# A gated sum of two attentions on one core: two turned operands, the weight loads, two scratch layouts and filling matmuls changed together

## The chip, the cores and the metric

The kernel runs on one core of a Trainium2 chip. The metric is the device time of one execution in microseconds (us). Three runs of the kernel before gave 1566.88, 1573.17 and 1576.6 us, so the median is 1573.17 us. The profiled execution took 1573.35 us; its span, from its first to its last instruction, is 1571.6 us.

## The reference, cut to what matters

Both attentions read the same x (2048 tokens of 576 values, bfloat16) and their results are mixed token by token by a gate g.

```python
# A: 32 heads of 128, 64 segments of 32 tokens, one after the other
for s in range(64):
    h = concat([mem, x[:, 32*s:32*s+32]])          # 8 + 32 = 40 rows
    q, k, v = h @ Wq, h @ Wk, h @ Wv                # 576 -> 32 x 128 each
    p = softmax(where(mask, q @ k.T * scale, -1e9))  # 40 x 40 per head
    o = (p @ v) @ Wo                                # 40 x 576
    mem = o[:, :8]                                  # the next segment needs this
    outs.append(o[:, 8:])
# B: full attention, 32 heads of 18, 2048 x 2048 scores per head
b = softmax(q_b @ k_b.T * scale_b) @ v_b @ wo
return g * a + (1 - g) * b                          # g = sigmoid((x * gate_w).sum(-1))
```

## The kernel before, in words

**The order of work.** Nothing is scheduled by the framework. Every piece of work is an `Op` with an engine (or a choice of two), an estimated duration, the pieces it depends on, a priority, and buffers ("tokens") that it takes and gives back. The class `Plan` (lines 45 to 204) runs a list scheduler over these estimates and emits the instructions of each engine in the order it finds. Its priorities are the numbers in `RANK` (line 17). On the chip each engine then works through its own list in order, and an instruction that waits holds up all behind it, on the queue of SP, which issues most DMAs, as well. The plan lets at most 8 DMAs of SP be under way at once.

**Start (before the segments).** x is loaded and turned on TensorE (`x_tile`). `project_qk` (line 532) and `project_v` (line 570) compute B's q, k and v, 36 and 32 products of five matmuls, and store them to DRAM scratch `qtd`, `ktd` and `vgd`; the store of v (line 597) writes pieces of 128 values. Meanwhile POOL issues the loads of A's three weight matrices, twelve groups of one 1024 KB and two 64 KB transfers (`load_w`, lines 477 to 486), each released by the end of the group before the last. `last_unit` (line 792) computes q, k and v of the last 8 tokens of 16 segments at a time, 24 units per 16 segments; the first 24 run before segment 0, the others among the segments. It stores q and k to `qkd` (line 844) in pieces of 32 values and v to `vld`.

**B.** 512 visits: one is 4 row-tiled score matmuls (`visit`, L708) into the only score buffer (4 PSUM banks), one exponential of 128 x 2048 on ScalarE (`expo`, L717), and 4 column-tiled matmuls (`values`, L726) that add to one open bank `ob` over 16 visits. `load_v` (line 671) brings the values back. At the end of the kernel function (lines 1393 to 1399) the visits beyond the first 23 are tied to segments, so that about 7.6 of them go with each.

**A segment.** `project` (line 1016) computes Q, K and V in two halves of 16 heads: six groups (called Q0, K0, Q1, K1, V0, V1 below) of 20 column-tiled matmuls (L1028). Each is copied from PSUM to a tile `tm` (128 x 512) by VectorE or ScalarE; there are four such tiles. For each half, `turn` (line 1082) transposes the Q and the K tile by 8 TensorE matmuls into a PSUM bank `pt`, and `ct` (line 1094) copies that bank to `qk` on VectorE. V is moved from `tm` to `v_sb` by 8 DMAs from SP (`put_v`, L1067). `ld_l` and `put_l` bring the last 8 tokens' q and k from `qkd` into `qk`. Then, per half: scores (`psh`, L1108), exponential on ScalarE, mask, sums, reciprocals, scaling on VectorE with small TensorE products between, values (`pso`, L1172), copies to `ot`, and `out_pieces` (L946), 64 small matmuls per half into `acc`. `ob_cast`, `ob_bd` and `fold` turn the 8 memory rows, and `put_h` (L1227) writes them into `ht` for the next segment: from one `put_h` to the next is the period of the recurrence. `put_o` (L1247, on POOL) collects the last 8 tokens for `last_out`, which multiplies those of four segments at once (again L946).

**End.** A's rows come back from DRAM, POOL multiplies them by g (L1349), TensorE multiplies B's result by its output weights (L1362), and VectorE joins the two.

Of the kernel before, what the change touches and what calls it, by code (L numbers as in the profile page):

```python
# [16 lines left out]
RANK = {  # L17
    "switch": 0.289, "near": 0.006, "early": 0.149, "wait": 0.21, "Q0": 1.449, "K0": 1.44, "Q1": 1.668,
    "K1": 1.703, "V0": 1.816, "V1": 1.981, "t0": 0.855, "t1": 0.104, "ph0": 2.493, "ph1": 1.947, "sm0": 1.698,
    "sm1": 1.765, "bc0": 1.404, "bc1": 1.296, "po0": 0.05, "po1": 0.541, "op0": 1.569, "op1": 0.05,  # L20
    "fo": 1.154, "lo0": 2.104, "lo1": 2.247, "la": 1.796, "ob": 1.008, "eQ": 0.456, "eK": 1.902, "eV": 1.335,
    "co": 3.82, "le": 6.051, "xp": 0.18, "mn": 0.857, "fin": 3.893, "la_gate": 1, "lo_gate": 1, "ahead": 23,
    "behind": 2, "tail": 0.042,
}
# [20 lines left out]
class Plan:  # L45
# [5 lines left out]
    SWITCH = 0.1  # L51

    def __init__(self):
        self.ops = []
        self.tokens = {}
        self.now = None
        self.lanes = [0.0] * self.LANES
        self.moved = 0.0

# [38 lines left out]
    def run(self):  # L98
# [12 lines left out]
        n = len(self.ops)  # L111
        best = {}
        dirty = set(free)
        while len(order) < n:
# [10 lines left out]
            est, op = best[pick]  # L125
            waiting_engs = op.engs
# [6 lines left out]
            if pick == "PE":  # L133
                if op.mode != mode:
                    dur += self.SWITCH
                mode = op.mode
            op.end = est + dur
# [78 lines left out]
def kernel(  # L216
# [68 lines left out]
    nc.vector.memset(cap[:], 3.0e38)  # L285
    nc.vector.memset(bsel[:], 0.0)
# [24 lines left out]
    vgd = dpool.tile([GB, P, NKB * P], BF16, name="vgd")  # L311
    otd = dpool.tile([Dm, S], BF16, name="otd")
    vld = dpool.tile([n_seg * LO, HD], BF16, name="vld")
    qkd = dpool.tile([n_seg // SG, P, SG, 2, H * LO], BF16, name="qkd")
# [22 lines left out]
    wo7 = bint.tile([P, Dm], BF16, name="wo7")  # L337
# [50 lines left out]
    z_w7 = zero("zw7", wo7[:], 0.6, 4.0)  # L388
# [83 lines left out]
    weight_loads = {}  # L472
    chain = [wbl[-1], wbl[-1]]
    for w, src, name in ((wv, A_Wv, "wv"), (wq, A_Wq, "wq"), (wk, A_Wk, "wk")):
        w2 = src.rearrange("d h e -> d (h e)")
        for c in range(NF):
            def load_w(e, w=w, w2=w2, c=c):
                nc.gpsimd.dma_start(out=w[0][:, c, :], in_=rows(w2, c))
                for two in range(2):
                    o = TL * two + TR * c  # L480
                    nc.gpsimd.dma_start(
                        out=w[1][o:o + TR, :],
                        in_=w2[RW * c + P:RW * c + RW, two * (HD // 2):(two + 1) * (HD // 2)],
                    )

            chain.append(add(f"{name}{c}", "POOL", 2.1, load_w, [chain[-2]], prio=0.15, tail=8.5))
        weight_loads[name] = chain[-4:]
# [8 lines left out]
    gwl = add("gw", "POOL", 5.0, load_gw, [chain[5]], prio=0.9, tail=3.0)  # L496
# [35 lines left out]
    def project_qk(which, m, t, prio):  # L532
# [20 lines left out]

        def st(e):
# [15 lines left out]
    def project_v(hf, kb, prio):  # L570
# [24 lines left out]

        def st(e):
            dma(
                out=vgd[:, :, :].rearrange("g p (k f) -> k p g f", f=P)[kb][:, hf * GB // 2:(hf + 1) * GB // 2, :],
                in_=vt[:, :, :].rearrange("p (g j) e -> p g (j e)", j=4),
            )  # L600

        v_stores[k] = add(f"vs{hf}{kb}", "SP", 0.4, st, [b], prio=0.8, dmas=1, kb=260)
# [29 lines left out]
    for m in range(1, 5):  # L632
# [3 lines left out]
        if m == 2:  # L636
            for kb in range(NKB):
                project_v(1, kb, 0.55)
    b_work = [o for o in plan.ops if o.name[:2] in ("pq", "pv", "ga", "xl", "xs")]
# [31 lines left out]
    def load_v(c):  # L671
# [4 lines left out]
        def fn(e):  # L676
            dma(out=vring[c % NVR][:, :], in_=vgd[g, :, kc * QC:(kc + 1) * QC])
# [13 lines left out]
    fin_state = {}  # L691

    for gq in range(GB * NQC):
        g, qc = divmod(gq, NQC)
        load_q(gq)
        for kb in range(NKB):
# [41 lines left out]
            if kb == 0:  # L738
                first_va = va
# [40 lines left out]

# [658 lines left out]
```

## Time and profile before

| | |
|---|---|
| profiled execution, its span | 1573.35 us, 1571.6 us |
| busy in the span: TensorE, ScalarE, VectorE, POOL | 1425.7 us (91%), 1066.2 us (68%), 764.9 us (49%), 194.4 us (12%) |
| mean granted TensorE clock | 0.961 of full speed |
| first and last start of a segment's projection matmul (L1028) | 168.8 us, 1524.8 us |
| median distance of two `put_h` (190.3 to 1514.2 us), smallest, largest | 21.2, 19.2, 24.2 us |
| DMA packets, of them under 512 B | 246877, 186487 |

The rows of groups in the profile give line, engine, operation, output and input tile, shape, number, then busy time and the mean ns of one, and then the idle time of the engine just before them with what ended it. The rows of stretches give, for a window of time, each engine's busy us and number of instructions, then the granted TensorE clock, the share of the DMA engines that were busy, and GB/s. The chain of waits gives start, length, and the engine and line that the end of the program was waiting for at that time; "issue" is time in which the profile shows no wait. Matmuls overlap, so a mean of 391 ns for one of four does not mean that four take 1.6 us.

### The profile page before, as it was taken

The numbers are of one execution on the slowest core, as the hardware profiler recorded it, in microseconds if no ns is written. First come the engines' busy times: TensorE is split into PE (matmuls) and PEld (weight loads), VectorE is DVE, ScalarE is ACT, GpSimd is POOL, SyncE is SP. The second block draws the span as 40 slices with busy tenths as digits, with TensorE's granted clock in tenths as the row PEclk, the third lists the DMA queues.
The fourth block names the chain that finished last, engine by engine and source line by source line (L and its number), as shares of the span: only waits on it lengthen the run. The fifth ranks groups of instructions, "written<-read, shape, count | busy, mean of one in ns | idle before, by whom it ended". The sixth has DMA issues, their size and how long they took to land.

```text
span 1571.6 us, 68445 instructions
## 1 busy us (share of the span) xinstructions
PE 1425.7 (91%) x30582; PEld 813.4 (52%) x30582; DVE 764.9 (49%) x1604; ACT 1066.2 (68%) x809; POOL 194.4 (12%) x523
## 2 busy tenths in 40 slices
PE   5398999999999999999999999999999898988996
PEld 3154545555554545555555555555555454555555
DVE  5154555544545454545554544555444545443454
ACT  2121788877777777777777777777776767766771
POOL 7301000000000000010000000000110100000025
PEclk9599999999999999999999999999999999998998
DMA  9957411212222111222221112212131111111033
GB/s 319 287 152 206 68 44 51 56 33 45 42 49 49 32 44 53 56 43 46 39 50 44 42 43 52 57 39 41 38 76 37 34 34 40 33 32 31 26 106 97
DMA packets 246877, 104.83 MB, mean 67 GB/s; under 512 B 186487, under 2 KB 242039, under 8 KB 245047
## 3 DMA queue, kind: packets, MB, share of 16 engines
q1 hardware_dynamic: 241591, 80.40, 21.2%
q0 software_dynamic: 3840, 18.88, 3.5%
q8 instruction: 239, 3.92, 1.0%
q10 hardware_dynamic: 1152, 1.18, 0.3%
q14 instruction: 55, 0.45, 0.1%
HBM read 52.74 MB, written 30.86 MB: 53 GB/s over the span
## 4 chain that ended last, share of the span: by engine, by line
PE 72%; ACT 10%; DMA 7%; issue 4%; SPq 3%; DVE 3%; POOL 1%; ACTq 0%; DVEq 0%; POOLq 0%
PE pvv L1028 24%; PE acc L946 11%; PE sb L708 10%; ACT etb L717 9%; PE ob L726 8%; PE pt L1087 4%; PE pv L807 4%; DMA v_sb<-tm 3%; SPq L1067 2%; PE pq L539 2%; PE pso L1172 2%; PE pv L803 2%; PE psh L1108 1%; POOL wv_m L1349 1%; PE prb L1151 1%
## 5 line engine op out<-in xcount | busy, mean ns | idle before, releaser
L717 ACT ACTIVATE etb<-sb 128x2048 bf16<-128x2048 f32 x512 | 961.3, 1878 | 386.3 <-PE sb L708 328.2
L363 DVE CAST tm<-pvv 128x512 bf16<-128x512 f32 x352 | 242.6, 690 | 285.2 <-PE pvv L1028 270.9
L1028 PEld LDWEIGHTS <-ht 128*32 128x32 bf16 x7680 | 199.5, 96 | 186.9 <-DVE ht L1227 23.8
L708 PE MATMUL sb<-qch,kch 32*128 32x512 bf16 x2048 | 208.6, 391 | 28.9 <-ACT etb L717 18.0
L726 PE MATMUL ob<-etb,vch 128*32 128x512 bf16 x2048 | 207.4, 396 | 0.8 <-ACT etb L717 0.7
L946 PE MATMUL acc<-wo,ot 128*32 128x144 bf16 x8192 | 167.7, 245 | 10.9 <-issue 10.7
L946 PEld LDWEIGHTS <-ot 128*32 128x32 bf16 x8192 | 157.1, 107 | 22.2 <-issue 17.2
L1028 PE MATMUL pvv<-wk_m,ht 128*32 128x512 bf16 x2048 | 140.8, 380 | 18.3 <-DVE ht L1227 18.2
L1028 PE MATMUL pvv<-wq_m,ht 128*32 128x512 bf16 x2048 | 144.4, 380 | 0.0
L708 PEld LDWEIGHTS <-kch 32*128 32x128 bf16 x2048 | 65.1, 91 | 139.9 <-issue 109.3
L1028 PE MATMUL pvv<-wv_m,ht 128*32 128x512 bf16 x2048 | 133.9, 379 | 0.0
L983 POOL COPY ht<-xg 128x96 bf16<-128x96 bf16 x64 | 17.1, 267 | 859.7 <-PE pvv L1028 843.2
L363 DVE CAST ot<-pso 128x320 bf16<-128x320 f32 x197 | 90.0, 485 | 65.1 <-PE pso L1172 64.8
L1095 DVE COPY qk<-pt 128x1024 bf16<-128x1024 bf16 x128 | 87.8, 686 | 53.8 <-PE pt L1087 53.5
L726 PEld LDWEIGHTS <-vch 128*32 128x32 bf16 x2048 | 54.3, 93 | 112.6 <-issue 105.0
L1203 DVE CAST obf<-acc 128x144 bf16<-128x144 f32 x64 | 19.7, 307 | 169.4 <-PE acc L946 169.2
L1087 PEld LDWEIGHTS <-tm 128*128 128x128 bf16 x1024 | 57.5, 98 | 45.5 <-issue 27.1
L1087 PE MATMUL pt<-ident,tm 128*128 128x128 bf16 x1024 | 79.4, 220 | 0.0
L1172 PE MATMUL pso<-et,v_sb 64*128 64x40 bf16 x2048 | 54.7, 179 | 26.0 <-DVE ot L363 16.8
L1161 DVE TENSOR_TENSOR et<-et,prb 128x320 bf16<-128x320 bf16 x128 | 57.2, 483 | 23.8 <-PE prb L1151 22.1
L1172 PEld LDWEIGHTS <-v_sb 64*128 64x128 bf16 x2048 | 38.8, 94 | 56.3 <-DMA v_sb<-tm 29.0
L1247 POOL COPY otl<-ot 128x256 bf16<-128x256 bf16 x64 | 26.2, 409 | 328.2 <-DVE ot L363 187.8
(128 smaller groups left out, 1523.1 us busy)
## 6 DMA issues: line engine op xcount, KB each, us to landing
v_sb<-tm SPq DMA_DIRECT2D x512, 32.0 KB
qkd<-vl SPq DMA_DIRECT2D x64, 128.0 KB
xl<-qkd SPq DMA_DIRECT2D x64, 128.0 KB
wo<-in_A_Wo_dram POOLq DMA_DIRECT2D x4, 1152.0 KB, 11.3
wv_m<-in_A_Wv_dram POOLq DMA_DIRECT2D x4, 1024.0 KB, 10.6
vgd<-vt SPq DMA_DIRECT2D x32, 128.0 KB
wq_m<-in_A_Wq_dram POOLq DMA_DIRECT2D x4, 1024.0 KB, 10.1
wk_m<-in_A_Wk_dram POOLq DMA_DIRECT2D x4, 1024.0 KB, 12.3
```

The costliest lines, as they stand in the source:

```text
L363: nc.vector.tensor_copy(out=out_of(), in_=in_of())
L539: nc.tensor.matmul(pq[:, :], lhsT=lw(c), rhs=xT[:, c, cs], start=(c == 0), stop=(c == NF))
L708: nc.tensor.matmul(sb[:, j, :], lhsT=kc[r, o:o + P], rhs=qt_[r, :], start=True, stop=True, tile_position=(32 * j, 0),)
L717: nc.scalar.activation(out=etb[:, :, :], in_=box["sb", gq, kb][:, :, :], func=ACT.Exp, scale=scale_b)
L726: nc.tensor.matmul(ob[32 * j:32 * j + 32, :], lhsT=vc[:, o + 32 * j:o + 32 * j + 32], rhs=etb[:, j, :], start=(kb == 0), stop=(kb == NKB - ...
L807: nc.tensor.matmul(pv[:, k * P:(k + 1) * P], lhsT=lw, rhs=xL[:, cc, cols], start=(c == 0), stop=(c == NF))
L946: nc.tensor.matmul(acc[32 * j:32 * j + 32, :], lhsT=o[:, slot, t0:t0 + CT], rhs=wo[:, h, RW * j:RW * j + RW], start=(first and s_ == 0), s ...
L1028: nc.tensor.matmul(pv[32 * j:32 * j + 32, :], lhsT=ht[:, cc, :], rhs=rw, start=(c == 0), stop=(c == NF), tile_position=(0, 32 * j), skip_g ...
L1087: nc.tensor.transpose(out=pt[:, a, :, i, :], in_=tm[:, i * Dh:(i + 1) * Dh], identity=ident[:, :])
L1095: nc.vector.tensor_copy(out=opened["qk"][:, hf, :, 0:16 * L].rearrange("p a (h t) -> p a h t", t=L)[:, :, :, 0:CT], in_=box["pt", s, hf][: ...
L1161: nc.vector.tensor_tensor(out=et[:, :], in0=et[:, :], in1=box["prb", s, hf][:, :], op=ALU.mult)
L1172: nc.tensor.matmul(ps[jj][:, r * L:(r + 1) * L], lhsT=v_sb[rr, hf * 1024 + r * Dh:hf * 1024 + (r + 1) * Dh], rhs=et[rr, r * L:(r + 1) * L] ...
```

## The change

1. **Turning.** The 8 matmuls of `turn` and the copy out of PSUM are replaced, for each of Q and K of each half, by one transposing DMA from SP (`tm` to a new tile `tt`, three of them) and one copy from `tt` to `qk` on VectorE or POOL. There are 4 DMAs and 4 copies in a segment where there were 16 matmuls and 2 copies. A `tm` tile is given back when its DMA is done.
2. **Weights.** The loads of A's weights and of its output weights are released one by one: each waits for a chosen copy of the B projections (or of the first `last_unit`s) through a small VectorE memset into its target.
3. **Scratch.** `vgd` and `qkd` are laid out so that each store writes 1 KB per partition; the load of `vch` then reads pieces of 128 values, and the load of `xl` pieces of 32 values, where they read 1 KB.
4. **Filling.** While `ob` is open, the planner puts a product of a zero tile with a tile of ones, added to `ob`, wherever its own timetable shows TensorE idle for at least 0.216 us (plus 0.1 us if the tiling changes): four column-tiled matmuls of 512 columns, or one full one.
5. **Around it.** All priorities have new numbers. The last block of B's output weights is loaded after the last Q instead of early. One buffer `otl` replaces two, and `last_out` for a group is planned ahead of the next group's `put_o`. `put_h` and `put_x` depend on all six groups of an earlier segment instead of V1 alone. Visits beyond 20 (before: 23) are tied to segments.

```diff
-    "switch": 0.289, "near": 0.006, "early": 0.149, "wait": 0.21, "Q0": 1.449, "K0": 1.44, "Q1": 1.668,
...
+    "switch": 0.401, "near": 0, "early": 0.353, "wait": 0.286, "Q0": 1.145, "K0": 1.449, "Q1": 1.603,
+    "K1": 1.589, "V0": 1.999, "V1": 4.037, "t0": 0.42, "t1": 0.05, "ph0": 6.405, "ph1": 0.336, "sm0": 1.963,
...
+            if pick == "PE" and open_ and self.warm is not None:
+                for m in ("col", "full"):
+                    if m not in (mode, op.mode):
+                        continue
+                    turn = 0.0 if mode == m else self.SWITCH
+                    done = sum(d for t, d in recent if t > free["PE"] - 2.5)
+                    if est - free["PE"] < self.WARM + turn + RANK["gap"] or done > RANK["cool"]:
+                        continue
+                    w = Op("warm", "PE", self.WARM, self.warm[m], [], 9.0, m, (), (), 0.0)
...
-    vgd = dpool.tile([GB, P, NKB * P], BF16, name="vgd")
+    vgd = dpool.tile([2, NKB, P, GB // 2, P], BF16, name="vgd")
...
-    qkd = dpool.tile([n_seg // SG, P, SG, 2, H * LO], BF16, name="qkd")
+    qkd = dpool.tile([n_seg // SG, 16, P, 512], BF16, name="qkd")
...
-            chain.append(add(f"{name}{c}", "POOL", 2.1, load_w, [chain[-2]], prio=0.15, tail=8.5))
+    def behind(name, beat, corner, n, fn, deps, tail):
+
+        mark = add(f"mk{name}", "DVE", 0.07, lambda e: nc.vector.memset(corner(), 0.0), [beat], prio=0.05)
+        before = paced[-1:]
+        op = add(name, "POOL", 0.7 * n, fn, [mark, *deps, *before], prio=0.15, tail=5.5)
...
+                    behind(f"{name}{c}", beats[2 + 5 * k], lambda w=w, c=c: w[0][0:1, c, 0:1], 3, load_w, [], 5.5)
...
-                out=vgd[:, :, :].rearrange("g p (k f) -> k p g f", f=P)[kb][:, hf * GB // 2:(hf + 1) * GB // 2, :],
-                in_=vt[:, :, :].rearrange("p (g j) e -> p g (j e)", j=4),
-            )
+                out=vgd[hf][kb].rearrange("p g f -> p (g f)"), in_=vt[:, :, :].rearrange("p h e -> p (h e)")
+            )
...
-            dma(out=vring[c % NVR][:, :], in_=vgd[g, :, kc * QC:(kc + 1) * QC])
+            dma(
+                out=vring[c % NVR][:, :].rearrange("p (k f) -> p k f", f=P),
+                in_=vgd[hf][4 * kc:4 * kc + 4][:, :, g % (GB // 2), :].rearrange("k p f -> p k f"),
+            )
...
+    def warm_col(e):
+        for j in range(4):
+            nc.tensor.matmul(
+                box["ob"][32 * j:32 * j + 32, :], lhsT=nil[:, 0:32], rhs=unit[:, :].unsqueeze(1).to_broadcast([P, 4, P]), start=False, stop=False,
+                tile_position=(0, 32 * j), skip_group_check=True,
+            )
...
-                o = (hf * 16 + j * 4) * LO
-                dma(
-                    out=qkd[q][:, :, kind, o:o + 4 * LO],
-                    in_=vl[:, :].rearrange("p (s f) -> p s f", s=SG),
-                )
...
+                dma(out=qkd[q][kind * 8 + hf * 4 + j], in_=vl[:, :])
...
-            dma(out=xl[:, :, :], in_=qkd[sq][:, si, :, :])
+            dma(
+                out=xl[:, :, :].rearrange("p a (u f) -> p (a u) f", f=4 * LO),
+                in_=qkd[sq][:, :, si * 4 * LO:(si + 1) * 4 * LO].rearrange("u p f -> p u f"),
+            )
...
-            def turn(e, hf=hf, s=s):
-                box["pt", s, hf] = pt = bank([P, 2, 4, 4, CT], BF16, "pt")
-                for a in range(2):
-                    tm = box["tm", s, a, hf]
-                    for i in range(4):
-                        nc.tensor.transpose(
-                            out=pt[:, a, :, i, :], in_=tm[:, i * Dh:(i + 1) * Dh], identity=ident[:, :]
-                        )
...
+            for a, ev_a in ((0, eq), (1, ek)):
+                def turn(e, hf=hf, s=s, a=a):
+                    box["tt", s, a, hf] = tt = given(opened["fix"], "tt", [P, 4, P], BF16)
+                    nc.sync.dma_start_transpose(out=tt[:, :, :], in_=box["tm", s, a, hf][:, :])
+
+                t_ = add(
+                    f"t{a}{hf}.{s}", "SP", 0.7, turn, [ev_a], prio=RANK[f"t{hf}"], take=("tt",),
+                    give=(("tm", ev_a, 0),), dmas=1, kb=128,
                 )
...
+                def ct(e, hf=hf, s=s, a=a):
+                    eng = nc.vector if e == "DVE" else nc.gpsimd
+                    eng.tensor_copy(
+                        out=opened["qk"][:, hf, a, 0:16 * L].rearrange("p (j i t) -> p j i t", i=4, t=L)[:, :, :, 0:CT],
+                        in_=box["tt", s, a, hf][:, :, :].rearrange("p i (j t) -> p j i t", t=CT),
+                    )
...
+                turned.append(add(
+                    f"ct{a}{hf}.{s}", ("DVE", "POOL"), (0.36, 0.85), ct, [t_, prev.get(f"psh{hf}")],
+                    prio=RANK["ct"], give=(("tt", t_, 0),),
+                ))
...
-        cur["otl"] = add(f"pt{s}", "POOL", 0.42, put_o, [*ots, group_end.get(s // 4 - 2)], prio=0.9)
+        cur["otl"] = add(f"pt{s}", "POOL", 0.42, put_o, [*ots, group_end.get(s // 4 - 1)], prio=0.9)
...
+    z_w7 = zero("zw7", wo7, 0.6, 0.6, [last["Q0"], last["Q1"]])
...
+    lw7 = add("lw7", "SP", 1.6, load_w7, [z_w7], prio=1.0, dmas=4, kb=90)
```

## The prediction

> **What bounds the kernel now.** First I read the slices and three stretches, to see in which stages a gain can lie at all.
>
> ```profile
> PE   5398999999999999999999999999999898988996
> ...
> PEclk9599999999999999999999999999999999998998
> DMA  9957411212222111222221112212131111111033
> ...
> 40.00:60.00 20.00, 7.96 (x41) 4.94 (x40) 3.35 (x7) 0.58 (x1) 10.30 (x20) 0.67 0.95 291
> 60.00:76.00 16.00, 3.72 (x12) 1.07 (x14) 1.30 (x3) 3.75 (x2) 2.01 (x4) 0.50 0.99 294
> ...
> 150.00:500.00 350.00, 330.76 (x7353) 190.05 (x7350) 177.43 (x361) 268.30 (x192) 27.77 (x92) 0.99 0.25 50
> 500.00:1200.00 700.00, 665.43 (x15369) 376.45 (x15365) 349.08 (x736) 530.18 (x400) 62.27 (x202) 0.99 0.21 47
> 1200.00:1500.00 300.00, 271.05 (x6173) 152.86 (x6170) 141.47 (x302) 211.83 (x152) 25.67 (x82) 0.93 0.12 32
> ```
>
> There are three regimes. Until about 85 us the DMA engines are full and TensorE starves. From 150 to 1200 us TensorE is 95% busy. After 1200 us, when no `last_unit` is left, it is 90% busy, at clock 0.93, and still a segment takes as long. Next I read the chain of waits over one late segment (`put_h` near 1339.3 and 1361.6 us), for what is last in it.
>
> ```profile
> 1343.77 0.55 PE pt L1087 x8
> ...
> 1347.90 0.55 PE pt L1087 x8
> ...
> 1352.48 0.34 SPq L1067
> 1352.82 0.04 issue
> 1352.86 0.59 SPq L1067
> ...
> 1353.49 0.59 SPq L1067
> 1354.08 0.04 issue
> 1354.13 1.86 DMA v_sb<-tm
> ```
>
> The first half, to the scores at 1350.1, is a row of TensorE work, both turns in it. Then the values wait for V: SP issues eight V stores, 1348.7 to 1354.7, and the last lands near 1356. So SP's issue rate already decides in each segment. Last the groups, for prices:
>
> ```profile
> L717 ACT ACTIVATE etb<-sb 128x2048 bf16<-128x2048 f32 x512 | 961.3, 1878 | 386.3 <-PE sb L708 328.2
> L1095 DVE COPY qk<-pt 128x1024 bf16<-128x1024 bf16 x128 | 87.8, 686 | 53.8 <-PE pt L1087 53.5
> L1087 PE MATMUL pt<-ident,tm 128*128 128x128 bf16 x1024 | 79.4, 220 | 0.0
> L1067 SPq DMA_DIRECT2D v_sb<-tm x512: 507/588/1834, 177.9 to 1530.3; - x171
> ```
>
> (The last row is that line's own view: min, median, max ns of one issue.) ScalarE needs 1.88 us a visit and 0.56 us until the next scores are there; 2.44 x 7.67 visits is 18.7 us a segment, below the 21.2 us (median) it takes. ScalarE is a second bound, not the first.
>
> [...] the 128 `acc` matmuls take 2.00 us in most segments and 3.84 us in some (1423 us). [...] weight loads after a change show 0.2 to 0.4 us of "issue". [...] In 60 to 76 us the engines are 99% busy at 294 GB/s, against 103% at 382 in 20 to 40[...]. [...]
>
> **The change part by part.** Times are against the profiled span, 1571.6 us; the profiled execution, 1573.35, is 1.75 above it and 0.2 above the median.
>
> *Weights and v stores (start).* B's projections run from 20 to 126.4 us. Their own work is 36 x 1.08 us + 32 x 0.61 us (five matmuls each, in stretches without stalls) = 58, with 2 us of gate products and about 12 visits x 0.75 = 9: 69 of 106 us, so 37 us are stalls. Named are 14.1 us (copies waiting for stores of q), 9.1 (stores of v) and half clock from 58 to 77 us. Pacing spreads the 14 MB of weights. DMA still has to move what it moves until 130 us: 31 MB (rates times lengths of the stretches); at the best stretch, 382 GB/s, 81 us. All but the last weights and later stores must fit into some 90 us, so not all 37 us come back. I take 25, bounds 10 and 37. The first `last_unit`s stall 4.7 us at 133 and run at half clock to 143.6 for 3 us more; I take 5 of these 8. The 16 early q and k stores go from 2048 pieces of 64 B to 128 of 1 KB. Start: -30, bounds -12 to -45. The moved pieces, 2048 of 64 B in each of 64 `xl` loads, are no more than the stores had; two `xl` tiles hide them, and without that cover they'd delay POOL's `put_l`, then the scores. The loads of `vch` (four times the pieces, 32 of them) have five buffers. The memsets (16 on VectorE, half idle) cost nothing.
>
> *Turns, TensorE's side.* 2 x 0.55 us a segment leave the chain, and about 0.4 us of tiling changes with them: 1.5 us x 64 = 96 us at most.
>
> *Turns, SP's side.* The trace has no transposing DMA. Issue: the plain DMA beside it, 0.59 us, is the low end. [...] I take 1.0. Landing: a V store takes 1.9 us; [...] I take 2.0; the high end is 5, as a 128 KB store in 64 B pieces held the chain for 4.6 us at 160 us. Per segment SP issues for about 11 to 12 of 21 us; four more at 1.0 make 16. Queued behind a turn on SP are the V stores, then loads of K, Q and `xl`, so this is where a new wait would come.
>
> Now the late segment again, from `put_h` = 0. Before: Q1 and K1 ready +7.4, V0 +8.4, V1 +10.7, scores +10.8 to 11.4, last V store issued +15.4, landed +16.7. After: Q1/K1 ready +6.8, V0 +7.9, V1 +9.2. K1's turn issues from +6, Q1's from +7.5 to +8.5 and lands +10.5; its copy is ready at +11.0. So the second half's scores come no earlier, while the first half's come at +9.2. V0's stores issue at +8.6 to +11.0 (4 x 0.59), V1's to +13.4, landed +15.3: 1.4 us earlier than before. That is the gain of a segment, set by V and not by the turns. At 0.59 us an issue it is the same (V0's copy limits), at 1.4 us about 1.0, and at 2.0 us none. In the middle segments TensorE is the bound and gives the same 1.5 us directly. ScalarE's 18.7 us and the plan's imperfect fit take some of it; I count 1.0 us x 64 = -64, bounds +20 and -95.
>
> *Copies.* 128 x 686 ns from PSUM become 256 from SBUF. Between 0.2 and 0.7 us on VectorE that is 51 to 180 us; VectorE, 49% busy, stays under 60%. On POOL one takes twice L997's 440 ns. On the path stands one of them in place of 0.69: nothing, hidden by V's stores.
>
> *Filling.* The clock lost is 0.01 in 1050 us and 0.07 in 300 us: 10 + 21 = 31 us if all of it were streaming. Much of that time TensorE is waiting anyway. A filler is 0.216 us (nine groups of four in 1.94 us); misplaced, with TensorE late against the plan, it costs that[...]. I take -10 net, bounds -25 and +40.
>
> *End.* The last 47 us are POOL's 1.7 us products, with the last `put_o` behind fourteen of them at 1548.7. The late load of the weight block (four small DMAs) has 30 us of cover. I take +3: bounds -10 and +12.
>
> Sum: -30 - 64 - 10 + 3 = -101, span 1470.6. The parts share one cover: TensorE time returned in late segments is the idle time that fillers use, and visits and segments must both speed up. I give back 15 for that: 1486, with 1.75 around it 1487.
>
> **The rivals.**
> *More comes through* (0.14): bounds near the good ends, -38 - 85 - 15, no give-back: 1435. For it: both of TensorE's stages shrink. Against: ScalarE's 18.7 us is then 1.2 us away.
> *Only the start pays* (0.25): a turn lands 5 us after its issue instead of 2, the second half's scores come at +14, 2.7 us of exponential, mask and scaling follow, the values start at +16.7 as before, and the period stays at 21.2. Then 1573 - 30 = 1543. For it: late segments have idle TensorE and are no shorter, so freeing it may buy nothing there.
> *The change doesn't do what it says* (0.08): the start stays DMA-bound, gaining 10, and fillers give that back: 1573, within 1%.
> *Slower, SP becomes the bound* (0.15): a turn holds SP for 2.8 us[...]. K1's turn ends +8.8, Q1's +11.6, V's stores +16.4, landed +18.3: +1.6 x 64 = 102, less 30: 1645. It decides from about 2.3 us, where 0.5 us a segment eats the start's 30 us. [...] For it: nothing here measures one.
>
> **How the numbers follow.** Likeliest 0.38: 1487, own range 1465 to 1510. About 1% (16 us) is what a measurement of this kernel tells from no change. Faster by more: 0.38 + 0.14 + 0.25 = 0.77. Within 1%: 0.08. Slower: 0.15. The range leaves out the slower rival and about 0.05 at the good end: 1435 to 1590.
>
> **What would show it.** Right: no stall near 33 to 47 and 60 to 75 us, first segment matmul near 139 us in place of 168.8; `put_h` 20.2 us apart; turns of about 1 us on SP; clock 0.98 or more after 1200 us. Wrong: waits of `psh` for `tt` or `qk`, V stores late because turns hold SP, a period over 21.2 us, fillers in stretches without idle TensorE, or `put_o` of the end later than before.

## The result, and the profile after

The changed kernel takes 1587.28 us (median of 4 runs, 1584.83 to 1588.85); the kernel before, beside it on the same chip, 1570.03 us (4 runs, 1566.36 to 1576.6). The ratio is 1.0104, with a 95% interval of 1.0062 to 1.0145: slower by about 1%, where 1487 us were forecast. The profiled execution took 1587.72 us, its span 1586.0 us.

First the same slices as before.

```profile
PE   7687899999999899999998998998998989899887
...
DMA  8767433332333333333333333333334322333243
```

The DMA row shows two changes. The first slices are less full (8, 7, 6, 7 in place of 9, 9, 5, 7), as the pacing meant them to be, and most later slices hold 3 in place of 1 or 2. Then the same stretches (columns: TensorE, weight loads, VectorE, ScalarE, POOL, granted clock, DMA share, GB/s).

```profile
40.00:60.00 20.00, 9.69 (x111) 5.81 (x112) 3.32 (x10) 5.63 (x3) 2.34 (x5) 0.71 0.76 227
60.00:76.00 16.00, 14.47 (x89) 6.13 (x87) 6.06 (x12) 2.06 (x2) 2.27 (x5) 0.83 0.68 203
150.00:500.00 350.00, 321.83 (x6991) 175.06 (x6984) 152.47 (x349) 259.10 (x192) 39.00 (x109) 0.97 0.37 77
500.00:1200.00 700.00, 652.67 (x15069) 356.35 (x15071) 326.63 (x763) 520.43 (x381) 83.27 (x231) 0.98 0.36 70
1200.00:1500.00 300.00, 270.87 (x6319) 141.71 (x6311) 137.94 (x333) 226.27 (x164) 32.58 (x98) 0.97 0.34 62
```

In 60 to 76 us TensorE is busy for 14.47 us where it was 3.72: the start's second stall went. In 40 to 60 us it is 9.69 where it was 7.96: there the stall mostly stayed. After 1200 us the clock is 0.97 in place of 0.93. In the two long stretches TensorE is *less* busy (321.83 and 652.67 us where it was 330.76 and 665.43), and yet the segments are no shorter. From the first `put_h` to the last it is 1324.2 us, and it was 1323.9; from the last `put_h` to the end 57.7, and it was 57.4. The whole difference is that the first `put_h` comes at 204.1 us and not at 190.3. So the change lost 14 us at the start and gained nothing in the 62 periods between. In them TensorE was busy for 1227.0 us and idle for 97.2; before it was 1241.8 and 82.1. The 15 us of work that the turns took off it came back as waiting.

The chain of waits of a late segment (`put_h` at 1341.23, the next at 1362.64) shows what stands where the turns on TensorE stood.

```profile
1347.93 5.54 DMA tt<-tm x2
...
1353.49 0.30 DVE qk L1169
...
1353.83 0.43 PE psh L1185 x16
```

In place of two pieces of 0.55 us of TensorE there is one wait of 5.54 us for turned tiles, then a copy, and then the second half's scores. It begins where TensorE's work on the path ends. The views of the two lines that SP issues (min, median, max ns of one):

```profile
L1160 SPq DMA_TRANSPOSE tt<-tm x256: 1188/1216/2428, 138.9 to 1537.6; - x128
```

```profile
L1141 SPq DMA_DIRECT2D v_sb<-tm x512: 507/588/1984, 158.7 to 1546.0; - x171
```

A turn holds SP for 1.22 us, twice a store of V (0.59). The group of the new copies on VectorE:

```profile
L1169 DVE COPY qk<-tt 128x512 bf16<-128x512 bf16 x191 | 58.1, 304 | 129.7 <-DMA tt<-tm 128.7 <-POOL qk L1071 0.6
```

A copy takes 0.30 us on VectorE, within what was expected; the 65 on POOL take 0.62, less than expected. What TensorE itself waits for in the segments is a copy of turned tiles ahead of the scores (`psh`) and V ahead of the values (`pso`); each row gives the sum in us, how many waits, and the longest:

```profile
PE psh L1185 <- DVE qk L1169: 20.1, 17, 2.8
PE pso L1249 <- DMA v_sb<-tm: 15.0, 27, 1.9
```

With 6.4 us more for copies on POOL that makes 41.5 us. A wait alone doesn't say what the time would be without it. That is what the runs are for.

### The profile page after: what moved, and what is told of

Same layout as the page of the kernel before. It is cut to its first block, busy times and chain, and to the rows that moved or that the text cites. A ratio compares the mean times of both kernels' runs of the same rounds, so it can differ in the third digit from the quotient of the medians.

```text
span 1586.0 us, 69008 instructions
## 1 busy us (share of the span) xinstructions
PE 1429.6 (90%) x30533; PEld 779.5 (49%) x30533; DVE 721.2 (45%) x1687; ACT 1070.9 (68%) x807; POOL 234.8 (15%) x588
## 3 DMA queue, kind: packets, MB, share of 16 engines
q1 hardware_dynamic: 380855, 113.99, 34.3%
## 4 chain that ended last, share of the span: by engine, by line
PE 55%; DMA 19%; ACT 9%; issue 6%; DVE 4%; SPq 4%; POOL 2%; ACTq 0%; DVEq 0%; POOLq 0%
PE pvv L1102 17%; DMA tt<-tm 10%; PE acc L1017 9%; ACT etb L788 8%; PE sb L779 8%; PE ob L797 6%; DMA v_sb<-tm 3%; SPq L1141 3%; PE pv L877 2%; PE ob L751 2%; PE pso L1249 2%; PE pv L873 2%; DMA qtd<-stg 1%; PE psh L1185 1%; DVE tm L400 1%
## 5 line engine op out<-in xcount | busy, mean ns | idle before, releaser
L400 DVE CAST tm<-pvv 128x512 bf16<-128x512 f32 x333 | 229.4, 690 | 250.1 <-PE pvv L1102 214.0
L1102 PEld LDWEIGHTS <-ht 128*32 128x32 bf16 x7680 | 209.3, 97 | 190.5 <-issue 16.3
L1017 PEld LDWEIGHTS <-ot 128*32 128x32 bf16 x8192 | 140.7, 99 | 23.1 <-issue 11.9
L1102 PE MATMUL pvv<-wv_m,ht 128*32 128x512 bf16 x2048 | 143.9, 383 | 9.0 <-DVE tm L400 5.4
L1169 DVE COPY qk<-tt 128x512 bf16<-128x512 bf16 x191 | 58.1, 304 | 129.7 <-DMA tt<-tm 128.7
L1169 POOL COPY qk<-tt 128x512 bf16<-128x512 bf16 x65 | 40.2, 620 | 390.4 <-DMA tt<-tm 389.9
L1185 PE MATMUL psh<-qk 128*64 128x40 bf16 x2048 | 56.0, 189 | 37.7 <-DVE qk L1169 20.1
L1185 PEld LDWEIGHTS <-qk 128*64 128x64 bf16 x2048 | 45.9, 113 | 78.2 <-issue 48.5
L1195 ACT ACTIVATE et<-psh 128x320 bf16<-128x320 f32 x128 | 55.7, 437 | 27.2 <-PE psh L1185 26.8
L400 DVE CAST vl<-pv 128x512 bf16<-128x512 f32 x84 | 57.6, 687 | 36.0 <-PE pv L877 18.1
## 6 DMA issues: line engine op xcount, KB each, us to landing
wo<-in_A_Wo_dram POOLq DMA_DIRECT2D x4, 1152.0 KB, 13.4
```

What stands on the lines that cost most here:

```text
L400: nc.vector.tensor_copy(out=out_of(), in_=in_of())
L1017: nc.tensor.matmul(acc[32 * j:32 * j + 32, :], lhsT=o[:, slot, t0:t0 + CT], rhs=wo[:, h, RW * j:RW * j + RW], start=(first and s_ == 0), s ...
L1102: nc.tensor.matmul(pv[32 * j:32 * j + 32, :], lhsT=ht[:, cc, :], rhs=rw, start=(c == 0), stop=(c == NF), tile_position=(0, 32 * j), skip_g ...
L1169: eng.tensor_copy(out=opened["qk"][:, hf, a, 0:16 * L].rearrange("p (j i t) -> p j i t", i=4, t=L)[:, :, :, 0:CT], in_=box["tt", s, a, hf] ...
L1185: nc.tensor.matmul(ph[64 * jj:64 * jj + 64, r * L:(r + 1) * L], lhsT=qk[:, hf, 1, k * L:k * L + 64], rhs=qk[:, hf, 0, k * L:(k + 1) * L], ...
L1195: nc.scalar.activation(out=opened["et", hf][:, :], in_=box["psh", s, hf][:, :], func=ACT.Exp, scale=scale_a)
```

## The experiments

In all kernels called "order kept" the planner's result is used unchanged, and only what one piece of work issues is altered (or one piece moved), so that every other instruction stands where it stood. In the others the planner made a new order. That matters: nearly the same edit, A's K weights ahead of `put_x`, gave 1608.24 us planned anew and 1590.85 us with the order kept. So some 17 us can come from the new order alone, and conclusions below rest on kept orders where there are any. Ratios are to the kernel before in the same batch of runs.

### What a turn costs in the segments

**Turns back on TensorE**, planned anew.

```diff
-                    nc.sync.dma_start_transpose(out=tt[:, :, :], in_=box["tm", s, a, hf][:, :])
+                    for i in range(4):
+                        nc.tensor.transpose(out=pt[:, a, :, i, :], in_=tm[:, i * Dh:(i + 1) * Dh], identity=ident[:, :])
```

> The changed kernel with the eight TensorE transposes and one PSUM copy per half put back in place of the transposing DMAs and their copies; all else as changed. Theory (a wait for the DMA has taken the place of the TensorE work, at about the same cost): from first to last put_h within 15 us of the changed kernel's 1324.1 us, time within 15 us of 1587. Rival A (the DMA turns do give about 1 us a segment, and fillers or priorities eat it): about 64 us slower, 1650. Rival B (the DMA turns are a loss and something else in the change a gain): below 1560.

Measured: 1616.18 us, ratio 1.0263 (1.0207 to 1.0319). First `put_h` at 191.5, from first to last 1360.3 us. The segments lie between the two answers and, planned anew, don't decide. Not expected: the start is 12.7 us earlier than with DMA turns.

**DMA turns in the kernel before**, planned anew (with the buffer edits that make room for three `tt` tiles), and with the order kept. In the second, both turns of a half are issued where the TensorE turn stood, into two `tt` tiles only, and VectorE makes all copies, so it is a harder case than the changed kernel.

```diff
+        nc.sync.dma_start_transpose(out=tt[:, :, :], in_=box["tm", s, a, hf][:, :])
-            nc.tensor.transpose(out=pt[:, a, :, i, :], in_=tm[:, i * Dh:(i + 1) * Dh], identity=ident[:, :])
```

> The kernel before with the transposing DMAs and their copies alone, plus the two buffer edits that make room for three tt tiles (one otl, the last block of B's output weights loaded late). Theory (wait replaces work): from first to last put_h within 15 us of the 1323.9 us before, time within 15 us of 1570. Rival A: about 64 us faster, 1506. Rival B: slower than 1590.

> The kernel before, order kept, with each turn issued as two transposing DMAs on SP at its place in the order and copied by two VectorE copies; two tt tiles, the last block of B's output weights loaded late to make room. Theory (wait replaces work, and TensorE that is left idle loses clock): from first to last put_h 1340 to 1385 in place of 1324, granted clock after 1200 us 0.90 or less. Rival A (the turns gain about 1 us a segment): 1275 or less. Rival B (the loss of the run planned with turns was its other plan): 1324 within 10.

Measured: planned anew 1642.5 us (1.0396, 1.032 to 1.0473), `put_h` 1385.2 us from first to last; order kept 1805.51 us (1.1467, 1.1429 to 1.1505), 1540.0 us. The first is Rival B's answer, the second is slower than any answer given. In neither are the turns a gain that something else ate: put into the old order they cost 3.5 us a segment, put into a new one 1.0 us, and only in the changed kernel's own tuned order are they even.

**No turn at all**, order kept: the copy reads `tm`.

```diff
-                    nc.sync.dma_start_transpose(out=tt[:, :, :], in_=box["tm", s, a, hf][:, :])
...
-                        in_=box["tt", s, a, hf][:, :, :].rearrange("p i (j t) -> p j i t", t=CT),
+                        in_=box["tm", s, a, hf][:, :].rearrange("p (i j t) -> p j i t", i=4, t=CT),
```

> The changed kernel, order kept, with the transposing DMAs left out: the copies read the tile tm itself, so Q and K of the first 32 rows go untransposed into the scores. Theory (the turn's issue and landing stand on the path of every segment): from first to last put_h 1265 or less in place of 1324, time 1530 or less. Rival (TensorE and ScalarE set the period and the turn is covered): from first to last put_h 1305 or more.

Measured: 1506.21 us (0.9559, 0.953 to 0.9587); from first to last `put_h` 1260.0 us, first `put_h` at 190.6. That is the theory's answer. Set beside the changed kernel's profiled span, the transposing DMAs cost 82 us: 64 in the segments, 14 before the first `put_h`, 4 after the last. The stretch from first to last `put_h`, the changed kernel first, then the one without turns:

```profile
204.14:1528.29 1324.15, 1227.00 (x28253) 663.41 (x28249) 613.45 (x1443) 995.36 (x728) 154.09 (x435) 0.98 0.35 67
```

```profile
190.55:1450.53 1259.98, 1205.00 (x28253) 652.86 (x28249) 613.08 (x1443) 991.45 (x728) 153.49 (x435) 1.00 0.22 45
```

So 42 of the 64 us are TensorE standing idle longer (97.2 us, not 55.0). The other 22 us are the same 28253 instructions done more slowly: the clock was granted at half for 51 us of this stretch, without turns for 10, and half of the difference, an estimate of what it cost, is about 20. Segment by segment (the order is the same, so the n-th can be set beside the n-th), 22 of 62 are over 1 us longer with turns, and they make up 56.2 of the 64.2 us. In those 22 SP spends 2.6 us on other DMAs ahead of V's first store, in the others 1.1: the cost falls where SP's queue is crowded.

**A plain DMA of the same bytes** in place of the transposing one, and **a transposing DMA that nothing reads**, order kept in both.

```diff
-                    nc.sync.dma_start_transpose(out=tt[:, :, :], in_=box["tm", s, a, hf][:, :])
+                    nc.sync.dma_start(out=tt[:, :, :].rearrange("p i f -> p (i f)"), in_=box["tm", s, a, hf][:, :])
```

> The changed kernel, order kept, with each transposing DMA replaced by a plain DMA of the same 128 KB from tm to tt, so Q and K of the first 32 rows go untransposed into the scores. Theory (a transposing DMA lands later than a plain one, which is what the prediction had priced at 2.0 us): from first to last put_h 1270 to 1290, time near 1525. Rival (any DMA on this path costs as much): 1310 or more, time 1570 or more.

> The changed kernel, order kept: the transposing DMAs are issued as before, but the copies read the tile tm itself and nothing reads what they write, so Q and K of the first 32 rows go untransposed into the scores. It keeps the turn's 1.2 us of SP queue and its load on the DMA engines, and takes away the wait for its landing. Theory (the landing is the cost): from first to last put_h 1260 to 1280, near the 1260.0 us without any turn. Rival (the time on SP's queue, with V's stores behind it, is the cost): 1300 or more.

Measured: plain 1526.8 us (0.967, 0.9628 to 0.9712), 1269.7 us from first to last `put_h`. Unread 1593.58 us (1.0108, 1.0051 to 1.0164), 1328.2 us. The first is as the theory said, the second is its failure: with nothing waiting for the landing, nothing is gained. The landing on the copies' path is therefore not what the turns cost by itself. Plain and transposing DMA differ in this on SP:

```profile
L1160 SPq DMA_DIRECT2D tt<-tm x256: 464/505/1240, 140.0 to 1476.9; - x128
```

0.505 us of SP in place of 1.216. One segment of the same number (the 37th), SP's queue in both kernels, first the changed one (start, length, line, what it issues, how many):

```profile
977.76 4.33 SPq L1160 DMA_TRANSPOSE tt<-tm  x3
982.14 1.57 SPq L702 DMA_DIRECT2D otd<-stage  x4
983.83 1.19 SPq L1160 DMA_TRANSPOSE tt<-tm  x1
985.06 5.83 SPq L1141 DMA_DIRECT2D v_sb<-tm  x8
```

```profile
946.34 2.52 SPq L1160 DMA_DIRECT2D tt<-tm  x3
948.92 1.59 SPq L702 DMA_DIRECT2D otd<-stage  x4
950.62 0.47 SPq L1160 DMA_DIRECT2D tt<-tm  x1
951.14 5.40 SPq L1141 DMA_DIRECT2D v_sb<-tm  x8
```

Four turns take 5.5 us of SP here where four plain DMAs take 3.0; the four small stores of `otd` in the middle are the same. V's stores begin 11.5 us after `put_h` (973.60) in the one, 9.0 us after it (942.17) in the other, and the segments take 23.4 and 19.2 us.

**V's second half stored from POOL**, order kept, in the changed kernel, in the kernel before, and in the changed kernel with unread turns as well.

```diff
-                    dma(
+                    (nc.gpsimd.dma_start if hf else dma)(
```

> The changed kernel, order kept, with the four stores of V's second half issued from POOL in place of SP. Theory (the turns' 1.22 us each on SP's queue push V's stores back, and the values wait for them): the last V store is issued 2 us earlier in a segment, from first to last put_h 1295 or less in place of 1324, time 1560 or less. Rival (the landing of the turns, and tm held until then, is the cost): from first to last put_h 1315 or more.

> The kernel before, order kept, with the four stores of V's second half issued from POOL in place of SP. Theory (V's stores are last in the kernel before as well, as its chain shows after 1200 us): from first to last put_h 1290 to 1312 in place of 1324, time 1540 to 1562. Rival (TensorE's work sets the kernel before, or POOL's queue delivers V later than SP's): 1320 or more.

> The changed kernel, order kept, with both earlier edits together: the transposing DMAs are issued but the copies read the untransposed tile tm, and V's second half is stored from POOL. Each alone left the segments at 1328.2 and 1316.4 us from first to last put_h. Theory (two paths of nearly equal length end at the values: turn, landing, copy, scores on one side, turns on SP's queue and then V's stores on the other; each covers the other): together 1265 to 1290, time 1515 to 1550. Rival (neither is the cost, for instance tm being held until the transposing DMA is done, or its load on the DMA engines): 1310 or more.

Measured: changed kernel 1584.91 us (1.007, 1.0043 to 1.0097), 1316.4 us from first to last `put_h`; kernel before 1570.51 us (0.9975, 0.9956 to 0.9994), 1317.5 us; both edits 1576.7 us (0.9994, 0.9971 to 1.0017), 1315.7 us. All three theories miss. The two runs of the changed kernel give the rival's answer, the kernel before lies between the two: by these answers neither V's second half on SP's queue, nor that and the landing together, is the cost. What TensorE waits for says what was left out. First the row for V in the kernel with no turn, then with the turn unread, then with both edits:

```profile
PE pso L1248 <- DMA v_sb<-tm: 6.6, 12, 2.0
```

```profile
PE pso L1249 <- DMA v_sb<-tm: 36.5, 60, 2.5
```

```profile
PE pso L1249 <- DMA v_sb<-tm: 33.5, 39, 5.5
```

In the changed kernel TensorE waited 26.5 us for copies and 15.0 for V. With the turn unread the waits for copies shrink to 1.5 us, but those for V grow to 36.5: the second path covers the first. With both edits the waits for V are still 33.5 us, and 27 us of that are for the *first* half: V's first half, still on SP, stands behind all four turns there as well. So this kernel didn't have the second path taken away, only half of it. The means over 62 segments, in us after `put_h`, worked out from each kernel's trace:

| kernel | last turn issued | last copy to `qk` done | last scores done | first store of V issued | last values done | next `put_h` |
|---|---|---|---|---|---|---|
| before (turns on TensorE) | 9.0 | 9.8 | 11.5 | 9.3 | 16.9 | 21.35 |
| changed | 9.4 | 11.5 | 12.3 | 9.7 | 17.8 | 21.36 |
| plain DMA | 7.7 | 10.4 | 11.6 | 8.6 | 16.9 | 20.48 |
| no turn | - | - | 11.4 | 8.4 | 16.8 | 20.32 |
| turn unread | 9.4 | - | 11.8 | 9.7 | 17.8 | 21.42 |
| V's second half from POOL | 9.2 | 11.3 | 12.1 | 9.5 | 17.6 | 21.23 |
| both edits | 9.3 | - | 11.7 | 9.6 | 17.5 | 21.22 |

V's first store and the values go with the period in all DMA kernels: 8.4 and 8.6 us with 20.3 and 20.5, 9.5 to 9.7 with 21.2 to 21.4. The scores do not: at 11.7 and 11.8 they are early in two of the slower kernels. This points to SP's queue, with V's first half behind the turns. Two rivals that the expectation of the kernel with both edits names can be held against the traces. If the turns' load on the DMA engines delayed V, its stores would take longer: from issue to landing they take 2.15 us on average in the changed kernel and 2.16 without turns. If `tm`, held until a turn is done, delayed V, its first half would reach `tm` late: it does so at +8.6 in place of +8.3, but then waits 1.1 us for its first store, in place of 0.1. A kernel with *all* of V's stores off SP's queue, which would prove it, was not tried.

### The fillers

**Without fillers**, planned anew, and with the order kept and the fillers just not issued; and **fillers in the kernel before**, where its own timetable, order kept, leaves TensorE idle. (The trace of the last shows 58 groups of four and 118 single full products, which is not the 87 groups of four that the expectations name; 232 + 118 products are about 87 times four.)

```diff
-    plan.warm = {"col": warm_col, "full": warm_full}
...
         for op in self.run():
+            if op.name == "warm":
+                continue
```

> The changed kernel without the filling products. Theory (fillers are of second order): time within 10 us of 1587; the granted clock after 1200 us falls from 0.97 towards 0.93. Rival A (fillers eat the turns' gain): 1540 or less. Rival C (fillers hold up the clock at a profit): 1600 or more.

> The changed kernel with its order of instructions kept on every engine, and only the filling products not issued. Theory (the fillers hold up the clock): 1600 to 1622, granted clock after 1200 us 0.92 or less. Rival (the 22 us that the run planned without fillers lost came from its other plan): within 8 us of 1587.

> The kernel before, its order kept, with filling products put where its own finished timetable leaves TensorE idle for 0.216 us or more while ob is open (87 groups of four). Theory (fillers hold up the clock, worth 18 us in the changed kernel, which had 225 groups of four and 75 full ones): 1555 to 1568, granted clock after 1200 us 0.95 or more. Rival (fillers gain only where the turns have left TensorE waiting): 1570 to 1585.

Measured: planned anew 1609.61 us (1.0218, 1.016 to 1.0277); order kept 1604.93 us (1.0182, 1.0145 to 1.0219); kernel before with fillers 1565.34 us (0.9916, 0.9892 to 0.994), clock 0.99 after 1200 us where it was 0.93. The stretch after 1200 us without fillers, order kept:

```profile
1200.00:1500.00 300.00, 262.12 (x5848) 144.19 (x5848) 131.10 (x319) 215.49 (x154) 30.46 (x92) 0.88 0.34 60
```

Clock 0.88 in place of 0.97. The fillers gain: about 12 us in the changed kernel by the two ratios (1.0182 less 1.0104, whose intervals touch, so the size is uncertain), 20 us by the profiled spans, 0.8% in the kernel before. That they are of second order, the theory of the run planned anew, was wrong.

### The start

**A's K weights ahead of `put_x`**, planned anew (one dependency more), then with the order kept.

```diff
-        lh = add(f"lh{s}", "POOL", 0.75, put_x, [lx, *(prev2.get(u) for u in UNITS)], prio=0.7, ...)
+        lh = add(f"lh{s}", "POOL", 0.75, put_x, [lx, *paced[8:12], *(prev2.get(u) for u in UNITS)], prio=0.7, ...)
```

> The changed kernel with one edit of order: put_x may be planned only after the last of the twelve weight loads, so that on POOL no load of A's K weights stands behind a put_x that waits for its xg load. Theory (the start loses by late K weights): the last wk load is issued near 115 us in place of 136.5, the K units no longer end at 178, first put_h at 190 to 196 in place of 204.2, time 1573 to 1579. Rival (the xl load in 64-byte pieces and the scratch stores behind the output weights set the start): first put_h stays at 202 to 206 and the time within 4 us of 1587.

> The changed kernel, order kept but for one move: on POOL the last two groups of A's K weights stand ahead of the first put_x. Theory (late K weights cost the start): those loads issue near 110 us in place of 135 to 137, first put_h 190 to 198 in place of 204.2, from first to last put_h 1324 within 6, time 1574 to 1582. Rival (turns ahead of the xl load on SP, and its 64-byte pieces, cost the start): first put_h 202 or later, time within 4 us of 1587.

Measured: planned anew 1608.24 us (1.0205, 1.0154 to 1.0255), order kept 1590.85 us (1.0108, 1.0056 to 1.016). First `put_h` at 198.2 and 198.1, outside the theory's ranges (to 196 and 198): about 6 us of the 14 come back, though in the second the segments took 9 us more (1333.4) and the time didn't fall. Six kernels that left the weights, layouts and turns of the start as changed had their first `put_h` between 200.1 and 207.2, so 6 us is little more than their spread.

**The 1 KB layout of `vgd` alone in the kernel before; the old layout of `qkd`, and the old weight loads, in the changed kernel.** The first two keep the order; the last is planned anew.

```diff
-    vgd = dpool.tile([GB, P, NKB * P], BF16, name="vgd")
+    vgd = dpool.tile([2, NKB, P, GB // 2, P], BF16, name="vgd")
```

```diff
-    qkd = dpool.tile([n_seg // SG, 16, P, 512], BF16, name="qkd")
+    qkd = dpool.tile([n_seg // SG, P, SG, 2, H * LO], BF16, name="qkd")
```

```diff
-                    behind(f"{name}{c}", beats[2 + 5 * k], lambda w=w, c=c: w[0][0:1, c, 0:1], 3, load_w, [], 5.5)
+            chain.append(add(f"{name}{c}", "POOL", 2.1, load_w, [chain[-2]], prio=0.15, tail=8.5))
```

> The kernel before, its order kept, with the 1 KB layout of vgd alone. The prediction's step (the 256-byte stores of v hold up the start): TensorE's stalls between 54 and 77 us go, first put_h 175 to 184 in place of 190.3, time 1560 to 1565. Rival (the start is bounded by the bytes that have to come in, or by the loads' order): first put_h 188 to 192, time within 5 us of the kernel before.

> The changed kernel, order kept, with the old layout of qkd: the stores write 64-byte pieces and the xl load reads 1 KB. Rival at the start (the xl load in 64-byte pieces, 7.6 us on the chain before the first scores, is the lost time): first put_h 195 to 199 in place of 204.2. Theory (turns and weights ahead of it in the queues are the lost time): first put_h 201 or later. From first to last put_h 1324 within 8 in both.

> The changed kernel with the weight loads of the kernel before (each group released by the end of the group before the last, output weights behind them). Its plan shifts, so only the start is read. The prediction's step (pacing is worth most of 25 us): first put_h 215 or later, stalls of TensorE between 30 and 75 us come back. Theory (pacing moves the wait from B's projections to A's K weights and gains nothing in sum): first put_h 198 to 208. Rival (pacing loses the start): 196 or earlier.

Measured: `vgd` alone 1579.17 us (1.0001, 0.9983 to 1.002), first `put_h` at 192.7, TensorE busy for 4.9 of 23 us between 54 and 77 us, where it was 5.5: no gain at all. Old `qkd` 1607.53 us (1.022, 1.0179 to 1.0261), first `put_h` at 208.0, and the segments 1341.6 us, 17 more than in the changed kernel: the 64-byte stores are no better at the start and dearer later, so the 1 KB stores are a gain. Old weights 1581.88 us (1.0044, 1.0023 to 1.0065), first `put_h` at 192.4: the rival was right, pacing loses the start, as far as a new order lets it be read.

### The version that the runs point to

The kernel before, its order kept, with the same fillers and V's second half stored from POOL.

> The kernel before, order kept, with the 87 groups of filling products and with V's second half stored from POOL: the two edits that did not lose. If their gains add (10 us and 4 us), 1560 to 1564 and faster than both kernels; if the filling alone matters or POOL's stores undo it, 1565 or more.

Measured: 1560.63 us (median of 6, 1557.06 to 1566.66; ratio 0.9878, 0.9844 to 0.9912), from first to last `put_h` 1308.0 us. The gains add, as the first answer had it. It is faster than both kernels, by 1.2% and about 2.2%.

## Why the prediction was wrong

**Turns, TensorE's side: the mechanism was right.** It said 1.5 us a segment off TensorE and V1 ready at +9.2. The last projection matmul ended at +9.2 (before: +10.7). The gain of 1.0 us a segment was there to be had: without any turn the segments took 64 us less than before, which is the forecast's own term. That the size fits is partly luck, as that kernel has new priorities as well, and fillers, which were worth 12 to 20 us of the whole.

**Turns, SP's side: the step that failed.** The issue was taken as 1.0 us, an estimate of the author's above the 0.59 of a plain store; 1.22 was measured. The landing was not the error: taken as 2.0 us after the issue, it came 1.2 us after it (median of all 256 turns; mean 1.6). The error is in the timetable of SP's queue. It had the last turn issue "from +7.5 to +8.5" and "V0's stores issue at +8.6 to +11.0 (4 x 0.59), V1's to +13.4". V0 was copied at +8.6, as forecast, but the last turn held SP from +8.1 to +9.4, and V's stores were issued from +9.7 to +15.2. The last landed at +16.7 in place of +15.3; before it was +16.2. The working let each of the last two turns start almost as soon as its tile was ready. In fact they started 0.9 us after it, because the queue was taken: from the first turn's start to the last one's end it is 6.5 us, of which the four turns hold SP for 5.3, and some of the rest goes to small loads and stores (`kch`, `qch`, `otd`, `a_dram`, up to 3.7 us in one segment), which the working had counted in the sum ("11 to 12 of 21 us") and placed nowhere.

For an issue of 1.4 us the working gave a gain of about 1.0; at 1.22 there was none. The same goes for the rival "SP becomes the bound": its mechanism is the one that the runs point to (its 2.8 us a turn was an assumption of the author's), but the working put the point without gain at 2.0 us a turn, and it was reached at 1.22. What stays open is how the 42 us of idle time divide between SP's time and the landing, as each covers the other: the landing and half of V's stores, taken away one by one or together, give back 9 us at most, while a plain DMA in the turn's place costs 10 us where a transposing one costs 64.

**Start: -30 forecast, +14 measured.** TensorE's work in two stretches, the kernel before first, then the changed one:

```profile
20.00:140.00 120.00, 83.38 (x507) 42.03 (x507) 42.12 (x76) 14.98 (x12) 28.08 (x58) 0.84 0.78 248
140.00:200.00 60.00, 56.26 (x961) 35.67 (x963) 28.93 (x54) 37.05 (x24) 3.63 (x14) 0.97 0.51 94
```

```profile
20.00:140.00 120.00, 96.47 (x661) 51.62 (x661) 47.70 (x102) 13.20 (x13) 27.12 (x63) 0.87 0.70 219
140.00:200.00 60.00, 45.47 (x643) 24.85 (x644) 16.22 (x33) 31.29 (x21) 4.12 (x9) 0.86 0.62 162
```

By 140 us the changed kernel is 13 us of TensorE work ahead, half of the 25 counted on, and the first segment matmul comes at 136.8 us (139 forecast, 168.8 before). From 140 to 200 it loses 11 again. The step that failed is that pacing returns stalls without moving them. POOL issues the weights, and what stands behind a wait in its queue waits as well, here 23.52 us:

```profile
109.03 0.98 POOL L528 DMA_DIRECT2D wk_t<-in_A_Wk_dram  x2
133.53 0.27 POOL L1054 COPY ht<-xg 128x96 bf16<-128x96 bf16 x1 [23.52 <-DMA xg<-xtd]
...
136.54 0.56 POOL L525 DMA_DIRECT2D wk_m<-in_A_Wk_dram  x1
```

The last two groups of A's K weights stood behind a `put_x` that waited 23.5 us for `xg`. With the output weights they came at 135 to 143 us, when the `last_unit` stores and the first turns wanted the DMA engines (share 0.96 in 140 to 160 us, before 0.77). Two pieces of the chain there:

```profile
142.55 12.20 DMA qkd<-vl
...
184.25 7.56 DMA xl<-qkd
```

A store of `qkd` took 12.2 us, and the first `xl` load, which has to wait for the K units, landed at 191.8. With the K weights moved up (order kept) it was the first turn that the start waited for:

```profile
141.00 11.97 DMA tt<-tm
```

Either alone cost little: old weights with DMA turns 192.4 and paced weights with TensorE turns 191.5 (both planned anew), paced weights with no turn 190.6 (order kept); both together 204.1. With plain DMAs in place of the turns it was 199.2, so much of the 14 us may not be peculiar to transposing; the spread named above is 7 us. The sum had added weights and turns as if they shared nothing; they meet in the same 20 us. That it is the DMA engines where they collide is read from the full share, and not separated by a run from SP's queue. The 1 KB stores of `vgd`, part of the -25, were worth nothing.

**Filling: -10 forecast**, -12 to -20 measured, inside the bounds. Fillers do hold up the clock: after 1200 us it is 0.88 without and 0.97 with them. The gap of 4.7 us at 133 us that the prediction read agrees with it: after it the clock was at half from 136.9 to 143.8 us. But the slow `acc` matmuls that it read at 1423 us are of another kind. The 3.84 us belong to 101 of the 128 (all of them took 4.05, at half clock), and no long gap stands before them: in the 5.00 us up to 1420.34, when the clock fell to half, TensorE was busy for 3.78 us, and no gap was over 0.71. So there the clock fell after short gaps alone, which fits that fillers in short gaps gain; that the gaps were the cause was not shown by itself. **End: +3 forecast**, +0.3 measured. **Copies: nothing**, as said; VectorE is at 45%. **Give-back of 15:** without object, as there was nothing to give back.

**The other rivals.** "Only the start pays" had the segments right (a period of 21.2, by late turns) and the start wrong; it had a landing of 5 us as the cause, where the median was 2.4. "Doesn't do what it says" came nearest in time, for another reason: parts of the change did work and were lost again.

## What to carry to other kernels

When work moves from an engine to a DMA queue, write down that queue instruction by instruction for one period, with everything that stands between and each instruction's own wait, before you price the move: the last in the queue pays, here the stores of V (the last landed at +16.7 us where +15.3 was forecast) as far as the traces show. A transfer that is paced must also be asked what it will meet when it comes late. And where TensorE is left idle in short gaps, products of zeros can be worth their price, as they were here: of the three parts that were put into the kernel before by themselves (turns, the layout of `vgd`, fillers) they alone gained (ratio 0.9916; the turns 1.0396 and 1.1467, the layout 1.0001).

## What the hardware showed that was not expected

A transposing DMA of 128 x 512 bfloat16 from SBUF to SBUF is not as fast as a plain one of the same 128 KB. It takes 1.216 us of SP's queue in place of 0.505, lands 2.44 us after its issue begins in place of 2.01 (medians of 256, from the semaphores of each DMA), and makes 544 packets in place of 144 (packets of the runs with, with plain and without turns, over 256). The share of the hardware queue is 34.3% of the span with transposing DMAs, 29.4% with plain ones and 23.1% without, which makes 0.77 us of all 16 engines for one turn and 0.40 for a plain one.

The granted clock fell to half though TensorE was far from idle. In the kernel before it did so at 1399.86, 1420.34 and 1444.23 us, and in the 5.00 us ahead of each TensorE was busy for 3.36, 3.78 and 3.21 us.
